# Transposing K loads of 3 MB instead of 1 MB, with another load order, in a two-problem attention kernel

## The chip, the cores and the metric

The kernel runs on one core of a Trainium2 chip. The metric is device time in microseconds (us); smaller is better. Ratios compare a kernel with the kernel before on the same chip in the same rounds, because the kernel before has a median of 1126.6 us on one chip and 1133.0 us on another. Where the text compares microseconds of two experiments, they may come from different chips.

A *unit* is one (batch, head) pair of one problem. There are 512 of them, 256 of problem A and then 256 of problem B. A *group* is four units. One group's K is 1 MB and its V is 1 MB.

## The reference, cut to what matters

```python
# two times (A, B) with B=16, Sq=144, D=448, H=16, Sk=512, Dh=256, bf16:
q = (x @ wq).reshape(B, Sq, H, Dh).transpose(0, 2, 1, 3)
scores = jnp.einsum("bhqd,bhkd->bhqk", q, k_cache) * (Dh ** -0.5)
p = softmax(scores, axis=-1)
o = jnp.einsum("bhqk,bhkd->bhqd", p, v_cache)
out = o.transpose(0, 2, 1, 3).reshape(B, Sq, H * Dh) @ wo
# the two outputs are concatenated along the last axis
```

The data are 134 MB of K and as much V, each byte used once, and some 19 MB of x, wq and wo.

## The kernel before: the parts that matter

One unit is eight matmuls for Q, eight for the scores S, an exponential on ScalarE, eight matmuls for PV, one for the row sums, and a normalization into a ring, from which the output projection (OP) takes chunks of 128 rows. TensorE works on Q of unit i+6, S of unit i+2 and PV of unit i in turn. All large loads are issued in order from one queue (SyncE, "SPq" in the profile):

```python
LQ, LS = 6, 2
WAVE = 4
NK, NV, NXG = 6, 5, 2                     # ring slots for K groups, V groups, x
kt_sb = sb("kt_sb", [128, NK, 8, UG * 128], BF16)

def t_load_k(G):                          # 1 MB: 512 rows of 1024, transposed by the DMA
    pr, r0 = divmod(UG * G, NU)
    sl = G % NK
    src = ks[pr].rearrange("b h (p c) d -> (b h p) (c d)", c=4)[r0 * 128:(r0 + UG) * 128, :]
    def e(q):
        return q.dma_start_transpose(kt_sb[:, sl, :, :], src).then_inc(sems["kt%d" % sl], 16)
    S.add(SP, e, writes=[(("kt", sl), G)], dma_sem="kt%d" % sl, name="k%d" % G)
# ... t_load_v(G): a plain 1 MB load into v_sb[:, G % NV]
# order: sorted by deadline. The first four groups one by one, then waves: K of four groups, then V of four.
for G in range(NG):
    lo = UG * (G - NK) + UG - 1 - LS + 1 if G >= NK else s_min     # when the slot is free
    w = 1 if G < WAVE else WAVE
    plan(lo, UG * (G - G % w) - LS, 0, 10 ** 6, t_load_k, G)
# ... the same for V, and for x, wq and wo by their deadlines
```

The columns of wq for problem B can be loaded only after the last Q of problem A that uses them, and wo of B only after the last output chunk of A. So about 7 MB of extra loads fall into the switch from A to B.

## Time and profile before

| | before |
|---|---|
| three runs without profile | 1123.84, 1124.79, 1131.62 us |
| profiled run | 1134.42 us (span 1132.7) |
| TensorE busy | 1050.6 us, 93% |
| undisturbed pace | 2.03 us per unit |

First the head of the profile page: the span, the engine table, and TensorE and the DMA engines in 40 slices of the span, each digit a busy share in tenths.

```profile
span 1132.7 us, 33125 instructions
...
PE 1050.6 (93%) x13952; PEld 925.9 (82%) x13952; DVE 657.6 (58%) x2183; ACT 621.8 (55%) x1573; POOL 643.4 (57%) x1065
...
PE   4857999999999999999969989999999999999995
...
DMA  9999999999999999999999999999999999999930
```

TensorE has two holes, the first 10% and the middle, where B begins. The DMA engines have none until the very end. Both are nearly full, so the question is which of them is waited for, and where. The waits view (total us, times, longest us) says that in the holes TensorE waits for DMA:

```profile
PE ot_ps L1007 <- DMA v_sb<-in_A_v_cache_dram: 22.1, 5, 12.7
PE qp_ps L937 <- DMA wq_sb<-in_A_wq_dram: 16.9, 3, 10.6
PE qp_ps L937 <- DMA wq_sb<-in_B_wq_dram: 10.9, 2, 7.4
...
PE ot_ps L1007 <- DMA v_sb<-in_B_v_cache_dram: 7.1, 3, 4.3
...
PE s_ps L961 <- DMA kt_sb<-in_A_k_cache_dram: 1.6, 1, 1.6
```

What a K load costs is seen in short windows. The last three columns are TensorE's granted clock, the DMA share and GB/s:

```profile
52.00:54.00 2.00, 2.00 (x35) 1.99 (x33) 1.41 (x6) 1.47 (x4) 1.38 (x3) 1.00 1.28 290
54.00:56.00 2.00, 0.91 (x12) 0.53 (x9) 1.51 (x5) 0.88 (x3) 1.38 (x3) 1.00 1.22 129
64.00:66.00 2.00, 0.00 (x0) 0.00 (x0) 0.00 (x0) 0.00 (x0) 0.00 (x0) 0.50 0.65 141
66.00:68.00 2.00, 0.00 (x0) 0.00 (x0) 0.00 (x0) 0.00 (x0) 0.00 (x0) 0.50 1.27 290
72.00:74.00 2.00, 0.62 (x6) 0.62 (x7) 0.00 (x0) 0.00 (x0) 0.00 (x0) 0.50 1.05 405
```

From 49.5 to 68.5 us four K loads run back to back. They move at 290 GB/s, but with windows between that move half of it: 4.8 us per load, where 1 MB at 290 GB/s would take 3.6. A share of the DMA near 1 does not tell these apart; the GB/s do. Plain V traffic (72 to 74 us) reaches 405. The clock of 0.50 is the other price of a long wait: eight matmuls took 1.14 us after it, 0.66 us otherwise. The Trainium skill ("TensorE: Matmul & The Clock Gate", Part 1: The HAM clock gate) says that an idle window brings the array to half clock; this trace agrees.

The queue's own timeline (start, length; issue times) shows those loads:

```profile
45.20 22.11 SPq L913 DMA_TRANSPOSE kt_sb<-in_A_k_cache_dram  x4
67.36 2.52 SPq L922 DMA_DIRECT2D v_sb<-in_A_v_cache_dram  x4
```

### The profile page before, as it was taken

The page shows a single profiled execution, that of the slowest core. Times are in us where ns is not written, and L with a number is a line of the kernel's source. Part 1 is how long each engine was busy: PE and PEld are TensorE (multiplying, and loading weights), DVE is VectorE, ACT ScalarE, POOL GpSimd, SP SyncE. Part 2 cuts the span into 40 slices and gives each one's busy share as a digit, 9 for nine tenths or more (in the row PEclk, how much of TensorE's full clock was granted, in tenths as well). Part 3 has the DMA queues.
Part 4 walks back from the last instruction along what each step waited for, and adds up shares of the span by engine and source line. Part 5 has one row for each costly group of instructions (what it writes and reads, how often), then busy time and mean ns, then how long its engine had stood idle before and what let it go on. Part 6 is the DMA issues. An engine that isn't in the chain of part 4 may idle for free.

```text
span 1132.7 us, 33125 instructions
## 1 busy us (share of the span) xinstructions
PE 1050.6 (93%) x13952; PEld 925.9 (82%) x13952; DVE 657.6 (58%) x2183; ACT 621.8 (55%) x1573; POOL 643.4 (57%) x1065
## 2 busy tenths in 40 slices
PE   4857999999999999999969989999999999999995
PEld 3756888888888888888858878888888888888883
DVE  2534566666656666666526645666656665666653
ACT  1534555665655555656525545666655555565552
POOL 1535456666656656666526645666656665666652
PEclk9879999999999999999979999999999999999998
DMA  9999999999999999999999999999999999999930
GB/s 239 255 310 258 267 285 273 279 275 285 256 270 262 277 274 264 261 270 240 268 309 282 254 270 265 284 279 283 229 262 263 281 274 282 283 264 261 264 121 12
DMA packets 629087, 294.21 MB, mean 260 GB/s; under 512 B 550464, under 2 KB 558656, under 8 KB 628928
## 3 DMA queue, kind: packets, MB, share of 16 engines
q1 hardware_dynamic: 627200, 287.86, 107.5%
q0 software_dynamic: 1728, 4.13, 1.0%
q8 instruction: 111, 1.82, 0.7%
q14 instruction: 48, 0.39, 0.1%
HBM read 148.90 MB, written 4.13 MB: 135 GB/s over the span
## 4 chain that ended last, share of the span: by engine, by line
PE 74%; DVE 7%; DMA 7%; SPq 6%; ACT 5%; issue 1%; POOLq 0%; POOL 0%; ACTq 0%
PE qp_ps L937 19%; PE op_ps L1098 18%; PE s_ps L961 18%; PE ot_ps L1007 16%; SPq L913 5%; ACT pt_sb L973 4%; DVE run_sb L1063 3%; DMA v_sb<-in_A_v_cache_dram 3%; DVE ring L1050 2%; DVE qt_sb L949 2%; PE ot_ps L1019 2%; DMA v_sb<-in_B_v_cache_dram 2%; DMA wq_sb<-in_B_wq_dram 1%; ACT ln_sb L1030 1%; DMA kt_sb<-in_A_k_cache_dram 1%
## 5 line engine op out<-in xcount | busy, mean ns | idle before, releaser
L982 POOL TENSOR_TENSOR pp_sb<-pt_sb 128x288 f32<-128x288 bf16 x512 | 374.3, 731 | 433.9 <-ACT pt_sb L973 433.0
L973 ACT ACTIVATE pt_sb<-s_ps 128x576 bf16<-128x576 f32 x512 | 333.4, 651 | 438.2 <-PE s_ps L961 438.1
L1063 DVE TENSOR_REDUCE run_sb<-ot_ps 1x1 bf16<-1x144 f32 x1024 | 262.2, 293 | 376.5 <-ACT ln_sb L1030 376.5
L937 PE MATMUL qp_ps<-xt_sb,wq_sb 128*128 128x144 bf16 x4096 | 347.3, 229 | 38.6 <-DMA wq_sb<-in_A_wq_dram 16.9
L937 PEld LDWEIGHTS qp_ps<-xt_sb,wq_sb 128*128 128x128 bf16 x4096 | 284.3, 99 | 113.2 <-issue 29.7
L1007 PE MATMUL ot_ps<-pt_sb,v_sb 128*128 128x144 bf16 x4096 | 344.1, 228 | 29.2 <-DMA v_sb<-in_A_v_cache_dram 22.1
L961 PE MATMUL s_ps<-qt_sb,kt_sb 128*128 128x144 bf16 x4096 | 344.6, 228 | 1.6 <-DMA kt_sb<-in_A_k_cache_dram 1.6
L1007 PEld LDWEIGHTS ot_ps<-pt_sb,v_sb 128*128 128x128 bf16 x4096 | 277.8, 99 | 31.1 <-DMA v_sb<-in_A_v_cache_dram 23.0
L961 PEld LDWEIGHTS s_ps<-qt_sb,kt_sb 128*128 128x128 bf16 x4096 | 278.5, 99 | 2.6 <-DMA kt_sb<-in_A_k_cache_dram 1.8
L949 DVE CAST qt_sb<-qp_ps 128x288 bf16<-128x288 f32 x512 | 225.5, 441 | 86.1 <-PE qp_ps L937 82.8
L986 POOL TENSOR_TENSOR ps_sb<-pp_sb 128x144 bf16<-128x144 f32 x512 | 250.6, 489 | 40.2
L1098 PE MATMUL op_ps<-wo_sb,ring 128*128 128x448 bf16 x1120 | 265.5, 353 | 0.5 <-DVE ring L1050 0.5
L1050 DVE TENSOR_TENSOR ring<-ot_ps,rinv_sb 128x288 bf16<-128x288 f32 (+8 forms) x640 | 231.0, 375 | 0.0
L1035 ACT ACTIVATE rinv_sb<-ln_sb 128x144 f32<-128x144 f32 x512 | 165.4, 323 | 16.1
L1030 ACT ACTIVATE ln_sb<-ot_ps 128x144 f32<-128x144 f32 x512 | 149.1, 291 | 35.0 <-PE ot_ps L1019 34.8
L1098 PEld LDWEIGHTS op_ps<-wo_sb,ring 128*128 128x128 bf16 x1120 | 98.2, 98 | 44.5 <-DVE ring L1050 1.1
L1019 PE MATMUL ot_ps<-ps_sb,ones 128*128 128x144 bf16 x512 | 116.3, 227 | 0.0
L1019 PEld LDWEIGHTS ot_ps<-ps_sb,ones 128*128 128x128 bf16 x512 | 50.5, 99 | 0.0
L1116 ACT ACTIVATE ost_sb<-op_ps 128x448 bf16<-128x448 f32 x35 | 18.6, 531 | 8.7 <-PE op_ps L1098 8.6
L1127 POOL DMA_DIRECT2D out_dram<-ost_sb x36 | 20.2, 561 | 4.3 <-ACT ost_sb L1116 4.1
L1098 PE MATMUL qp_ps<-wo_sb,ring 128*128 128x448 bf16 x32 | 7.2, 352 | 0.0
L1098 PEld LDWEIGHTS qp_ps<-wo_sb,ring 128*128 128x128 bf16 x32 | 3.1, 98 | 2.9
(13 smaller groups left out, 6.1 us busy)
## 6 DMA issues: line engine op xcount, KB each, us to landing
v_sb<-in_A_v_cache_dram SPq DMA_DIRECT2D x64, 1024.0 KB, 9.6
v_sb<-in_B_v_cache_dram SPq DMA_DIRECT2D x64, 1024.0 KB, 10.1
out_dram<-ost_sb POOLq DMA_DIRECT2D x36, 112.0 KB, 4.8
wo_sb<-in_A_wo_dram SPq DMA_DIRECT2D x8, 448.0 KB, 9.1
wo_sb<-in_B_wo_dram SPq DMA_DIRECT2D x8, 448.0 KB, 5.0
wq_sb<-in_A_wq_dram SPq DMA_DIRECT2D x4, 768.0 KB, 5.6
wq_sb<-in_B_wq_dram SPq DMA_DIRECT2D x4, 768.0 KB, 14.0
kt_sb<-in_A_k_cache_dram SPq DMA_TRANSPOSE x64, 7.9
```

What stands on the lines that cost most here:

```text
L937: ins = t.matmul(qp_ps[:, dc * SQ:(dc + 1) * SQ], lhsT=wq_sb[:, kc, c0:c0 + 128], rhs=xt_sb[:, xsl, kc, xo:xo + SQ], start=(kc == 0 and dc ...
L949: return v.tensor_copy(qt_sb[:, sl, :, :], src)
L961: ins = t.matmul(s_ps[bank][:, c // 2, (c % 2) * SQ:(c % 2 + 1) * SQ], lhsT=kt_sb[:, ksl, 2 * c + dc, jj * 128:(jj + 1) * 128], rhs=qt_sb[ ...
L973: return a.activation(pt_sb[:, psl, :, :].rearrange("p (a b) q -> p a (b q)", a=2), s_ps[bank][:, :, 0:2 * SQ], AF.Exp, scale=DH ** -0.5)
L982: return g.tensor_tensor(pp_sb[:, sl, :, :], pt_sb[:, psl, 0:2, :], pt_sb[:, psl, 2:4, :], op=ALU.add)
L986: return g.tensor_tensor(ps_sb[:, sl, :], pp_sb[:, sl, 0, :], pp_sb[:, sl, 1, :], op=ALU.add)
L1007: ins = t.matmul(ot_ps[ob][:, dc * SQ:(dc + 1) * SQ], lhsT=v_sb[:, vsl, j, c * DH + dc * 128:c * DH + (dc + 1) * 128], rhs=pt_sb[:, sl, c, ...
L1019: return t.matmul(ot_ps[ob][:, 2 * SQ:3 * SQ], lhsT=ones[:, :], rhs=ps_sb[:, sl, :], start=True, stop=True)
L1035: return a.activation(rinv_sb[:, sl, :], ln, AF.Exp, scale=-1.0)
L1050: ins = v.tensor_tensor(ring[:, 2 * h:2 * h + 2, r0:r0 + q1 - q0], ot_ps[ob][:, 0:2 * SQ].rearrange("p (c q) -> p c q", c=2)[:, :, q0:q1], ...
L1063: return v.tensor_reduce(run_sb[0:1, k, U:U + 1], ot_ps[ob][0:1, 2 * SQ:3 * SQ], axis=AX.X, op=op)
L1098: ins = t.matmul(acc[0:m, 0:D], lhsT=ring[:, c, col0:col0 + m], rhs=wo_sb[:, c, :], start=(c == first), stop=(c == last))
```

## The change

K of up to three groups comes in one transposing load of 3 MB. The layout of `kt_sb` changes so that the slots lie side by side along the free dimension. Each such load is followed by the V loads of the same groups, with wq between them where it is due. The intent is fewer K loads and a better order at the switch. The turns from K to V traffic do not become fewer: in the steady stretch they come every 12 units instead of every 16.

```diff
-    WAVE = 4
+    WAVE, NKD = 3, 4
-        kt_sb = sb("kt_sb", [128, NK, 8, UG * 128], BF16)
+        kt_sb = sb("kt_sb", [128, 8, NK * UG * 128], BF16)
-        def t_load_k(G):
+        def t_load_k(G, m):
-            src = ks[pr].rearrange("b h (p c) d -> (b h p) (c d)", c=4)[r0 * 128:(r0 + UG) * 128, :]
+            src = ks[pr].rearrange("b h (p c) d -> (b h p) (c d)", c=4)[r0 * 128:(r0 + m * UG) * 128, :]
+            sem = "kt%d" % (k_index[G] % NKD)
-                return q.dma_start_transpose(kt_sb[:, sl, :, :], src).then_inc(sems["kt%d" % sl], 16)
+                return q.dma_start_transpose(kt_sb[:, :, sl * UG * 128:(sl + m) * UG * 128], src).then_inc(
+                    sems[sem], 16)
# ... matmul operand and semaphores to match; the sorting by deadline goes, and instead:
+        while G < NG:
+            n = min(WAVE, NG - G)
+            # ... x, when it is due
+            while g < G + n:
+                m = min(G + n - g, NK - g % NK, GPP - g % GPP)
+                k_index[g] = len(k_index)
+                plan(t_load_k, g, m)
+                g += m
+            for g in range(G, G + n):
+                pr, gl = divmod(g, GPP)
+                if gl < HG:
+                    plan(t_load_wq, pr, gl)
+                plan(t_load_v, g)
+                if pr == 0 and gl == WAVE * 2 - 1:
+                    for wg in range(NWG):
+                        plan(t_load_wo, 0, wg)
+            G += n
```

More of the change, by code (lines that the diff above doesn't have):

```diff
@@ L839, in bass_concat_heads__mha_block_cached__gqa_block_cached__near_ridge_kernel @@
         sem_names = list(COMPUTE)
-        for i in range(NK):
+        for i in range(NKD):
             sem_names.append("kt%d" % i)
@@ L905, in t_load_x @@
             S.add(SP, e, writes=[(("xt", sl), XG)], dma_sem="xt%d" % sl, n_dma=2, name="x%d" % XG)
-        def t_load_k(G):
+        def t_load_k(G, m):
             pr, r0 = divmod(UG * G, NU)
             sl = G % NK
-            src = ks[pr].rearrange("b h (p c) d -> (b h p) (c d)", c=4)[r0 * 128:(r0 + UG) * 128, :]
+            src = ks[pr].rearrange("b h (p c) d -> (b h p) (c d)", c=4)[r0 * 128:(r0 + m * UG) * 128, :]
+            sem = "kt%d" % (k_index[G] % NKD)
             def e(q):
-                return q.dma_start_transpose(kt_sb[:, sl, :, :], src).then_inc(sems["kt%d" % sl], 16)
-            S.add(SP, e, writes=[(("kt", sl), G)], dma_sem="kt%d" % sl, name="k%d" % G)
+                return q.dma_start_transpose(kt_sb[:, :, sl * UG * 128:(sl + m) * UG * 128], src).then_inc(
+                    sems[sem], 16)
+            S.add(SP, e, writes=[(("kt", sl + j), G + j) for j in range(m)], dma_sem=sem, name="k%d" % G)
         def t_load_v(G):
@@ L961, in e @@
                         ins = t.matmul(s_ps[bank][:, c // 2, (c % 2) * SQ:(c % 2 + 1) * SQ],
-                                       lhsT=kt_sb[:, ksl, 2 * c + dc, jj * 128:(jj + 1) * 128],
+                                       lhsT=kt_sb[:, 2 * c + dc, (ksl * UG + jj) * 128:(ksl * UG + jj + 1) * 128],
                                        rhs=qt_sb[:, U % NQT, dc, :], start=(dc == 0), stop=(dc == 1))
@@ L1131, in bass_concat_heads__mha_block_cached__gqa_block_cached__near_ridge_kernel @@
         t_init()
+        s_min = -LQ - 24
         dma_plan = []
-        def plan(lo, deadline, phase, lead, fn, *args):
-            dma_plan.append((deadline, phase, len(dma_plan), lo, lead, fn, args))
-        s_min = -LQ - 24
-        def wave(G):
-            return UG * (G - G % WAVE)
-        for XG in range(NXGT):
-            pr, j = divmod(XG, Bn // XB)
-            u_first = pr * NU + j * XB * H
-            if XG >= NXG:
-                pr0, j0 = divmod(XG - NXG, Bn // XB)
-                lo = pr0 * NU + (j0 + 1) * XB * H - 1 - LQ + 1
+        _at = [s_min]
@@ new lines, in plan @@
+        def plan(fn, *args):
+            if fn is t_load_x:
+                XG = args[0]
+                pr0, j0 = divmod(XG - NXG, Bn // XB)
+                lo = pr0 * NU + (j0 + 1) * XB * H - LQ if XG >= NXG else s_min
+            elif fn is t_load_wq:
+                pr, hg = args
+                lo = pr * NU - H + 4 * hg + 4 - LQ if pr > 0 else s_min
+            elif fn is t_load_k:
+                lo = UG * (args[0] + args[1] - NK) - LS if args[0] + args[1] > NK else s_min
+            elif fn is t_load_v:
+                lo = UG * (args[0] - NV + 1) if args[0] >= NV else s_min
@@ L1148, in bass_concat_heads__mha_block_cached__gqa_block_cached__near_ridge_kernel @@
             else:
                 lo = s_min
-            plan(lo, u_first - LQ - 16, 0, 10 ** 6, t_load_x, XG)
-        for pr in range(NP):
-            for hg in range(HG):
-                dl = pr * NU + 4 * hg - LQ
-                lo = pr * NU - H + 4 * hg + 3 - LQ + 1 if pr > 0 else s_min
-                plan(lo, dl, 1, 10 ** 6, t_load_wq, pr, hg)
-        for wg in range(NWG):
-            plan(s_min, OP_START - 12 + wg, 2, 10 ** 6, t_load_wo, 0, wg)
-        for G in range(NG):
-            lo = UG * (G - NK) + UG - 1 - LS + 1 if G >= NK else s_min
-            w = 1 if G < WAVE else WAVE
-            plan(lo, UG * (G - G % w) - LS, 0, 10 ** 6, t_load_k, G)
@@ L1162, in bass_concat_heads__mha_block_cached__gqa_block_cached__near_ridge_kernel @@
-        for G in range(NG):
-            lo = UG * (G - NV) + UG - 1 + 1 if G >= NV else s_min
-            w = 1 if G < WAVE else WAVE
-            plan(lo, UG * (G - G % w) - LS, 1, 10 ** 6, t_load_v, G)
-        dma_plan.sort(key=lambda t: t[:3])
-        _prev = s_min
-        _tmp = []
-        for dl, ph, sq, lo, lead, fn, args in dma_plan:
-            _prev = max(_prev, lo, dl - lead)
-            _tmp.append((_prev, dl, sq, fn, args))
-        dma_plan = _tmp
+            _at[0] = max(_at[0], lo)
@@ new lines, in plan @@
+            dma_plan.append((_at[0], fn, args))
+        k_index = {}
+        GPP = NG // NP
+        x_next = 0
+        G = 0
+        while G < NG:
+            n = min(WAVE, NG - G)
+            while x_next < NXGT and UG * (G + n) > x_next * XB * H - H:
+                plan(t_load_x, x_next)
+                x_next += 1
+            g = G
+            while g < G + n:
[12 more added lines that the diff above has]
+            G += n
@@ L1210, in bass_concat_heads__mha_block_cached__gqa_block_cached__near_ridge_kernel @@
             while dma_plan and dma_plan[0][0] <= i:
-                _sl, _dl, _sq, fn, args = dma_plan.pop(0)
+                _lo, fn, args = dma_plan.pop(0)
                 fn(*args)
```

## The prediction

> **What bounds the kernel now.** Two resources nearly tie. TensorE is busy 1050.6 of 1132.7 us (engine table). Undisturbed, by the starts of the 512 exponentials (one per unit), units 64 to 152 take 178.5 us and 320 to 456 take 276.9: 2.03 us per unit. DMA needs almost as long. In windows of 2 us, transposing traffic peaks at 290 GB/s (3.6 us per 1 MB K load), but in four back-to-back K loads from 49.5 to 68.5 us each takes about 4.8 us: 1.1 us of near-silence per load. V runs at 370 to 400 GB/s, 2.7 us per load; a switch from K to V costs about 2 us. A wave of 16 units is 4x4.8 + 4x2.7 + 2 = 32 us of DMA against 32.5 of TensorE. Any extra load (x, wq, wo) becomes a TensorE wait.
>
> Waits (wait view): V 29.2 us, wq 27.8 (10.6 is the start), K 1.6; 29.7 more is put down to issue. Two places lose: the first 120 us (12.7 us at 61, 6.5 at 108, 4.6 at 26), and 532 to 694 us, where units 232 to 344 take 252.9 us against 227: wq of problem B stands behind slot-bound K loads, V behind wo.
>
> **What the change does.** The bytes stay. Two thirds of the per-load gaps go: 3 MB should take 3x3.6 + 1.1 = 12 us instead of 14.3, if 290 GB/s holds inside one load. A wave of 12 units then needs 12 + 8.2 + 2 = 22 us against 24.4 of TensorE: 10% DMA slack instead of 2%. The Trainium skill ("DMA: Bandwidth & Descriptors", Latency and other measured facts) has 261 GB/s for a non-contiguous DMA transpose; this trace's 290 within a load decides.
>
> Price: the first wq now stands behind 3 MB of K, until about 22 us: the first Q moves from 10.6 to 22 us, the first exponential from 20.7 to 30; unit 12's Q waits for the fourth wq until about 54 us. The waits at 61 and 108 us go. Exponential 40 starts near 122 us instead of 129.9: 8 us gained.
>
> At the switch to B, wq is laid between single V loads; one 5 us wait is left (third wq behind 3 MB of K), so 19 us gained. Smaller V waits (142, 270, 815 us) go: 1 us. The pace of 2.03 us and the tail stay: TensorE's.
>
> **Sum.** 1124.8 - 8 - 19 - 1 = 1097; leaning towards a worse start, 1100 us. Range 1078 to 1120. Chances: faster over 2% 0.58, within 2% 0.38, slower 0.04.
>
> **What would show it.** 3 MB K loads landing in about 13 us, transposing traffic flat at 290 GB/s. First Q near 22 us, first exponential near 30, a wait for wq until about 54, exponential 40 near 122. Units 232 to 344 in about 234 us. V waits below 5 us in total. Units 64 to 152 still 178 us.
>
> **What would make it wrong.** The 1.1 us gaps recur within a 3 MB load (14 to 15 us each): no slack, the start 10 us worse, near 1115. Or slots freed 12 units at a time stall K: my margin is 24 us against 12 to 15. After long waits TensorE's clock falls (0.56 from 62 to 73 us; eight matmuls then took 1.14 instead of 0.66 us; the skill's "TensorE: Matmul & The Clock Gate", Part 1, ties it to idle windows): fewer, longer waits move a few us. The switch may stall on wo, which shares K's queue.

## The result, and the profile after

| | before | after |
|---|---|---|
| runs | 1123.84, 1124.79, 1128.40, 1131.62 us | 1112.11, 1112.30, 1113.43, 1113.96 us |
| median | 1126.6 us | 1112.87 us |
| ratio | | 0.9874 (95%: 0.9834 to 0.9913) |

The kernel is 1.3% faster: inside the range of the prediction, but within 2%, where I had put the larger chance on more. That it lies inside owes much to a range of 42 us: of the 28 us that I had summed up, half came. On another chip, against before's 1131.5 us, the same kernel had 1113.4 us and a ratio of 0.9835 (0.9777 to 0.9892). The kernel after is also steadier: its eight runs span 4.4 us, the kernel before's seven on that second chip alone span 11.

The head of the page after:

```profile
span 1112.2 us, 33041 instructions
...
PE 1044.0 (94%) x13952; PEld 920.7 (83%) x13952; DVE 657.3 (59%) x2183; ACT 620.2 (56%) x1573; POOL 642.2 (58%) x1065
...
PE   1698999999999999999969999999999999999995
...
DMA  9999999999999999999999999999999999999930
```

The waits view after:

```profile
PE qp_ps L939 <- DMA wq_sb<-in_A_wq_dram: 32.5, 2, 22.7
...
PE qp_ps L939 <- DMA wq_sb<-in_B_wq_dram: 9.6, 1, 9.6
...
PE s_ps L963 <- DMA kt_sb<-in_A_k_cache_dram: 3.2, 1, 3.2
...
PE op_ps L1100 <- DMA wo_sb<-in_B_wo_dram: 0.8, 1, 0.8
```

No wait for V is left. All waits of TensorE for DMA together were 58.6 us before and 46.1 us after (55.0 and 46.0 in the second profiles shown below). One long wait at the start has become longer (22.7 us, the first wq behind 3 MB of K), one of 9.6 us at the switch remains. The windows after show what a 3 MB load looks like:

```profile
12.00:14.00 2.00, 0.00 (x0) 0.00 (x0) 0.00 (x0) 0.00 (x0) 0.00 (x0) 1.00 1.28 290
14.00:16.00 2.00, 0.00 (x0) 0.00 (x0) 0.00 (x0) 0.00 (x0) 0.00 (x0) 1.00 1.28 290
38.00:40.00 2.00, 2.00 (x35) 1.99 (x33) 1.41 (x6) 1.34 (x4) 1.39 (x3) 1.00 2.14 275
40.00:42.00 2.00, 1.91 (x31) 1.72 (x28) 1.64 (x6) 1.35 (x4) 1.51 (x3) 1.00 0.53 116
42.00:44.00 2.00, 1.75 (x29) 1.56 (x26) 1.24 (x4) 1.61 (x5) 1.26 (x3) 1.00 1.27 290
```

The first load runs flat at 290 GB/s. The second (35 to 48 us) has a silence in its middle, at 40 us, where no load begins or ends. That was not in my picture, and it is taken up below.

To see where the time went I use the start of each unit's exponential (one instruction per unit, 512 in all). Two profiles of each kernel are shown; the second of before is the first experiment, the second of after comes from the second chip. Times are us from the span's start.

| exponential of unit | before | before, 2nd | after | after, 2nd |
|---|---|---|---|---|
| 0 | 20.7 | 21.9 | 31.6 | 30.8 |
| 40 | 129.9 | 130.3 | 126.2 | 123.6 |
| 64 | 177.2 | 177.2 | 173.1 | 170.5 |
| 232 | 517.8 | 517.7 | 512.8 | 510.3 |
| 344 | 770.7 | 764.7 | 752.1 | 750.7 |
| 511 | 1115.0 | 1108.9 | 1095.7 | 1094.3 |
| span | 1132.7 | 1125.6 | 1112.2 | 1111.6 |

From the second profile of before to the first of after the span falls by 13.4 us (the medians fall by 13.7): 4.1 us by unit 64, 0.8 us from 64 to 232, 7.7 us from 232 to 344 (the switch: 247.0 to 239.3), 0.6 us from 344 to 511, and 0.2 us after. The pace of the undisturbed stretches does not move: units 64 to 152 take 178.3 us in that second profile of before and 177.5 in after.

### The profile page after: what moved, and what is told of

Read it like the earlier page. It is cut to its first block, busy times and chain, and to the rows that moved or that the text cites. A ratio compares the mean times of both kernels' runs of the same rounds, so it can differ in the third digit from the quotient of the medians.

```text
span 1112.2 us, 33041 instructions
## 1 busy us (share of the span) xinstructions
PE 1044.0 (94%) x13952; PEld 920.7 (83%) x13952; DVE 657.3 (59%) x2183; ACT 620.2 (56%) x1573; POOL 642.2 (58%) x1065
## 4 chain that ended last, share of the span: by engine, by line
PE 76%; DVE 8%; ACT 6%; SPq 4%; DMA 4%; issue 1%; POOLq 0%; POOL 0%; ACTq 0%
PE qp_ps L939 20%; PE s_ps L963 19%; PE op_ps L1100 19%; PE ot_ps L1009 16%; ACT pt_sb L975 4%; SPq L914 3%; DVE run_sb L1065 3%; DVE ring L1052 2%; DVE qt_sb L951 2%; PE ot_ps L1021 2%; DMA kt_sb<-in_A_k_cache_dram 2%; ACT ln_sb L1032 1%; DMA wo_sb<-in_B_wo_dram 1%; DMA wq_sb<-in_A_wq_dram 1%; DMA wq_sb<-in_B_wq_dram 0%
```

## The experiments

Eleven runs were made, nine of them of changed kernels; all gave correct results. Two ideas for more lookahead were not run. A ring of eight K slots with 4 MB loads does not fit into the on-chip memory SBUF (the build stops at `qt_sb`: 3456 bytes needed where 2912 were left). With fewer V slots and a shorter output ring it fitted, but then an output chunk was overwritten before it was read, and the kernel did not build.

### The kernel before, once more

No edit.

> The kernel before, unchanged, for a second profile. The first profile ran 1134.4 us, 8 to 10 us over the median of the unprofiled runs. Theory: the kernel before sits on a tie of DMA and TensorE, so its waits for V around 640 to 700 us (4.3 + 2.3 us) and after the x loads come and go from run to run; this profile then shows 1124 to 1128 us and fewer such waits. Rival: the profile itself costs some 8 us; then this one is near 1134 too.

It took 1127.37 us, with a profile of 1125.6 us, against 1127.4 to 1136.7 us of the unprofiled runs on its chip. So the profile does not cost 8 us, and the rival is out. The waits of this profile:

```profile
PE ot_ps L1007 <- DMA v_sb<-in_A_v_cache_dram: 19.6, 3, 12.4
PE qp_ps L937 <- DMA wq_sb<-in_B_wq_dram: 9.8, 2, 6.6
...
PE ot_ps L1007 <- DMA v_sb<-in_B_v_cache_dram: 4.4, 2, 3.8
```

The V waits of A and B are 24.0 us instead of 29.2, and units 232 to 344 took 247.0 us instead of 252.9. The first profile was of one of the less lucky runs of a kernel whose time wanders, and I had subtracted what I saw in it from the median of others.

### Order without size

```diff
-                plan(t_load_k, g, m)
+                plan(None, g, m)              # only advances the time, as for the 3 MB load
+                for j in range(m):
+                    k_index[g + j] = len(k_index)
+                    plan(t_load_k, g + j, 1)
# ... NKD = 6 semaphores, and plan(None, ...) enters no load
```

> The kernel after with each 3 MB K load cut into three 1 MB loads back to back, all else and the order unchanged. Theory A (each K load has a fixed 1.1 us of silence, so size gives the DMA slack): three loads take 14.3 us where one took 12, DMA needs 24.5 us per 12 units against TensorE's 24.4, V or K waits come back in the steady stretch and the start is 5 to 10 us worse: 1120 us or more. Theory B (the silences come from instruction fetches that fall into transposing traffic, whatever the load size, and the gain comes from the order of the loads alone): 1113 us, and the V waits stay at zero.

It took 1125.9 us (1124.3 to 1130.4), ratio to before 0.9955 (0.9909 to 1.0000). Theory B falls: the order alone is worth 0.45%, and by the interval between nothing and 0.9%. The profile (1125.6 us) shows that it trades: unit 64 comes at 171.6 us, 5.6 us earlier than in the kernel before, but units 232 to 344 take 249.1 us against 247.0, and units 344 to 511 346.6 against 344.2. V and wo waits are back:

```profile
PE qp_ps L939 <- DMA wq_sb<-in_B_wq_dram: 11.1, 1, 11.1
...
PE op_ps L1100 <- DMA wo_sb<-in_B_wo_dram: 3.4, 2, 1.9
...
PE ot_ps L1009 <- DMA v_sb<-in_B_v_cache_dram: 2.8, 2, 2.4
PE ot_ps L1009 <- DMA v_sb<-in_A_v_cache_dram: 2.5, 2, 1.4
```

The start, though, is no worse than with 3 MB loads (171.6 against 173.1 and 170.5), so the part of theory A that had it 5 to 10 us worse falls too. One thing is not quite equal: the first of three small loads may start when its own slot is free, a large one only when all three are. That favours the small loads, and they lose all the same.

### Size without order

The kernel before, its order kept, with the layout of after and 2 MB loads in the waves:

```diff
-            plan(lo, UG * (G - G % w) - LS, 0, 10 ** 6, t_load_k, G)
+            m = 1 if G < WAVE else 2
+            if G % m:
+                continue
+            lo = UG * (G + m - NK) - LS if G + m > NK else s_min
+            plan(lo, UG * (G - G % w) - LS, 0, 10 ** 6, t_load_k, G, m)
```

> The kernel before with the order of before, but the K loads of a wave of 16 units in two 2 MB loads instead of four 1 MB loads. Theory A: two fixed silences of 1.1 us per wave fewer, 4 to 8 us faster than before (1118 to 1122). Theory B: same as before within its spread (1124 to 1130); the wait for wq of problem B stays over 10 us in both.

It took 1115.0 us (1114.7 to 1115.3), ratio 0.9855 (0.9819 to 0.9891). This is 16 to 18 us, more than twice the 4 to 8 us that theory A had asked for; why it is so much more stays open. Merging pairs of loads in the old order gives, within the intervals, what the whole change gives. With the run before, which had the new layout but small loads, this settles the main question: the gain comes from the size of the K loads. TensorE's waits for DMA agree: 55.1 us together with the order alone, 39.0 us with the size alone.

```profile
PE s_ps L962 <- DMA kt_sb<-in_A_k_cache_dram: 8.0, 2, 5.6
...
PE ot_ps L1008 <- DMA v_sb<-in_A_v_cache_dram: 5.9, 3, 4.7
PE qp_ps L938 <- DMA wq_sb<-in_B_wq_dram: 5.9, 2, 3.9
...
PE ot_ps L1008 <- DMA v_sb<-in_B_v_cache_dram: 2.2, 1, 2.2
```

The wait for wq of B fell to 5.9 us, although I had expected it to stay over 10. I read this as wq arriving earlier, because the K loads ahead of it take less DMA time.

What a load takes, from the trace's packet records (first to last packet of each K load that started after 120 us; worked out from the records, not a line of a view):

| kernel | size | loads | mean us | median us |
|---|---|---|---|---|
| before | 1 MB | 116 | 4.99 | 4.98 |
| order without size | 1 MB | 116 | 5.01 | 4.98 |
| size without order | 2 MB | 58 | 9.37 | 9.24 |
| after | 3 MB | 36 | 13.39 | 13.04 |

A line through the means of 1 and 3 MB (5.01 and 13.39) is 4.19 us per MB and 0.82 us per load; it gives 9.2 us for 2 MB. So a 3 MB load saves 2 x 0.82 = 1.6 us, not 2.3 us as I had it. The 0.82 us are a fit, and not all of it need be the load's own. With small loads in the new order, the 14 loads with no instruction-fetch packet (see below) from 0.5 us before their start to their end took 4.1 us on average, the 72 with one took 5.2 us. A short load meets fewer packets anyway, so the split stays open.

The K loads begun after 120 us take 588 us together with small loads in the new order, and 510 us in the kernel after. Part of this shows as a quiet load queue. In steps of 0.2 us in which the packets that begin on it carry less than 10 GB/s, it is quiet for 16.4 us between 120 and 520 us with small loads in the new order, and for 29.8 us in the kernel after; between 700 and 1040 us it is 14.2 and 24.6 us. (Packets still under way do not count here: with the bytes of all queues spread over each packet's duration, 0.0 and 8.6, and 0.2 and 7.6 us are left.) The last load's data end at 1087.3 and 1064.1 us. Only 13 us of all that reach the time, since TensorE sets the pace in between.

### The wq loads of B before the large K load

```diff
-                if gl < HG:
+                if gl < HG and (pr == 0 or g < G0 + 2):
                     plan(t_load_wq, pr, gl)
                 plan(t_load_v, g)
+                if g == G0 + 1:
+                    for hg in range(2, HG):
+                        plan(t_load_wq, 1, hg)
```

> The kernel after with the third and fourth wq load of problem B put before the 3 MB K load of units 264 to 275 instead of behind it. Theory: the wait of 9.6 us at 577 us and the slow clock after it go, about 12 us faster than after: 1101 us; units 256 to 264 take 16 us instead of 28.2. Rival: the K load, 6 us later, becomes the next wait and half of it is given back: 1106 us.

It took 1111.5 us (1110.2 to 1114.2), ratio 0.9832 (0.9792 to 0.9871); the kernel after, unchanged, has 0.9874 and 0.9835 on its two chips. So this is the same as after: not only the theory fell but the rival as well, as more than half was given back. The wait for wq is gone, and others have come:

```profile
PE s_ps L963 <- DMA kt_sb<-in_B_k_cache_dram: 4.7, 2, 3.3
...
PE s_ps L963 <- DMA kt_sb<-in_A_k_cache_dram: 3.8, 1, 3.8
...
PE op_ps L1100 <- DMA wo_sb<-in_B_wo_dram: 2.6, 1, 2.6
```

Units 256 to 264 took 20.4 us instead of 28.2, but units 232 to 344 took 238.2 us, against 240.4 us in the second profile of after. Moving one load in a crowded queue moved the wait.

### The kernel after on the second chip, and added instructions

The second profile of after was taken with two kernels that carry some 12,500 instructions more. These are waits on a semaphore that has long passed, after the first 60 instructions of each engine. They do nothing but must be fetched. (12,500 was my count beforehand. The traces have 40,024 instructions instead of 33,041 and 40,108 instead of 33,125, so 6,983 more.)

```diff
+        PAD = {ACT: 3, DVE: 2, POOL: 4}
+                    for _ in range(PAD.get(eng_name, 0)):
+                        eng.wait_ge(table[PE], 1)
```

> The kernel after, unchanged, on the same chip as the other runs of this job: 1111 to 1115 us. In its trace the 3 MB K loads take 13.0 us (median, first to last packet).

It took 1113.4 us (1112.6 to 1116.5); the 3 MB loads had a median of 13.2 us and a mean of 13.38.

> The kernel after with some 12,500 more instructions (waits on a semaphore that has long passed, on ScalarE, VectorE and GpSimd), which do nothing but have to be fetched. Theory (each 16 KB instruction fetch stops transposing traffic for about 1.3 us, which is part of what I took for a fixed cost per load): some 40 to 50 more fetch packets, and a 3 MB K load takes 13.5 us or more instead of 13.0. Its time stays within 10 us of after, as after has DMA slack outside the start and the switch. Rival (fetches only coincide with the silences): K loads stay at 13.0 us.

> The same added instructions in the kernel with 1 MB loads, which has no DMA slack. Theory: K loads go from 4.9 to 5.1 us or more each, and the time rises by more than in the kernel after, to over 1135 us. Rival: 1124 to 1131 us as without them.

The reason for this pair is the silence at 40 us. The packet records of the kernel after show packets of 16 KB on the instruction queues, and where one falls into transposing traffic, that traffic goes silent shortly after. Of the 45 such packets that began well inside a K load (0.3 us after its start or later, 1.5 us before its end or earlier), all 45 were followed within 1.2 us by a silence of 0.5 us or more (transposing packets begun at under 40 GB/s); of 11 packets of 8 KB, 6 were. The first 130 us have four cases of 16 KB:

```
16 KB instruction packet at 39.4  77.4  99.45 120.78 us
silence of transposing traffic from 39.9 (1.3), 77.9 (1.2), 99.9 (1.4), 121.2 (1.4) us
```

The queue table of the second profile of after, then of the one with more instructions (packets, MB, share):

```profile
q8 instruction: 111, 1.82, 0.7%
q14 instruction: 48, 0.39, 0.1%
```

```profile
q8 instruction: 111, 1.82, 0.6%
q14 instruction: 103, 0.84, 0.2%
```

There are 55 more packets, all of 8 KB on queue 14; the 16 KB packets stay at 111. So this tests the small packets, and for the large ones there is only the coincidence in time. The fetch packets per 3 MB load (from its first packet to the end of its last) rise from 1.89 to 2.97 (mean), and the load from 13.38 to 14.08 us (median 13.2 to 13.7). Within the padded kernel, loads with one fetch take 12.8 us (median of 5), with two 13.7 (6), with three 13.7 (13), with four 15.0 (9). A fetch more in a 3 MB load thus goes with some 0.65 us more. Each side is one run, but this side of the theory held.

The other did not. In the kernel with 1 MB loads, fetches per load rose from 0.85 to 1.32 by the same count, but the mean load went only from 5.01 to 5.07 us, less than expected. Nor do the times say what I wanted: 1131.7 and 1141.0 us, 18 and 15 us above their bases (the second base is a median from another chip), the first far beyond the 10 us that I had allowed. The added instructions slowed the undisturbed stretch as well (units 64 to 152: 181.0 us against 177.6 in the second profile of after), so these times say nothing about DMA. What the runs show is that large transposing loads were longer where more fetches fell into them. How much of the time before the change was due to them stays open.

### Another start

```diff
-            n = min(WAVE, NG - G)
+            n = min(1 if G < WAVE else WAVE, NG - G)
+                if g == WAVE:
+                    plan(t_load_wq, 0, WAVE)        # the fourth wq ahead of the fourth K group
-                if gl < HG:
+                if gl < HG and g != WAVE:
-                if pr == 0 and gl == WAVE * 2 - 1:
+                if pr == 0 and gl == WAVE * 3 - 1:  # wo three groups later
```

> The kernel after with another start: the first three groups in 1 MB K loads, each followed by its wq and V, the fourth wq before the fourth K load, and wo of problem A behind the ninth V instead of behind the sixth. Theory: the first Q is back at 10.6 us and the wait for the fourth wq goes; then DMA bounds the first 120 us, and exponential 64 starts 3 to 8 us earlier than after's 173 us: 1105 to 1110 us. Rival: the start is DMA-bound whatever the order, exponential 64 stays at 171 to 173 us and the time at 1112 us.

It took 1113.05 us (1112.5 to 1114.9), the kernel after 1113.36 on the same chip: the rival was right. The first exponential came at 27.1 us and exponential 40 at 118.8 us, 4.8 us ahead of the second profile of after. By exponential 64 nothing was left: 170.5 us in both. K waits took it:

```profile
PE qp_ps L939 <- DMA wq_sb<-in_A_wq_dram: 23.2, 3, 14.5
...
PE s_ps L963 <- DMA kt_sb<-in_A_k_cache_dram: 9.6, 4, 4.2
```

My reading is that the start depends on how long the DMA needs for what the first 64 units use, and that this comes out the same in these two orders.

### wo of B later

On top of the moved wq loads, four loads of wo from unit 270 and four from unit 282, and the first output chunk of B begun at unit 290:

```diff
-                            queue_chunk(r, max(i + OP_DELAY, OP_START))
+                            queue_chunk(r, max(i + OP_DELAY, OP_START + pr * (NU + 4)))
+            while wo_free and i >= NU + (14 if wo_n < 4 else 26):
+                t_load_wo(1, wo_free.pop(0))
+                wo_n += 1
```

> The kernel with wq of problem B moved ahead (as in s3), and besides wo of problem B loaded later: four loads from unit 270, four from unit 282 on, with the first output chunk of B begun at unit 290 instead of 273. Theory (the switch is bound by the sum of DMA work that falls into it, so that moving one load only moves the wait; spreading it into later slack is what helps): units 240 to 320 take 6 us less than the 176.3 us of after: 1105 to 1108 us. Rival: what is put off is missed later, by unit 344 nothing is gained: 1111 us as s3.

It took 1112.8 us (1111.4 to 1116.4), ratio 0.9863 (0.9819 to 0.9908): the rival. Units 240 to 320 took 175.7 us, in the second profile of after 176.3. No order that I tried at the switch made it shorter by more than about 2 us.

### Where along the run the size pays

Small loads everywhere but in groups 48 to 83, and the reverse:

```diff
-                k_index[g] = len(k_index)
-                plan(t_load_k, g, m)
+                plan(None, g, m)                      # only advances the time, as above
+                st = 1 if not 48 <= G < 84 else m     # and the reverse: 48 <= G < 84
+                for j in range(0, m, st):
+                    k_index[g + j] = len(k_index)
+                    plan(t_load_k, g + j, st)
```

> The kernel after with 1 MB K loads everywhere but in groups 48 to 83 (units 192 to 335, around the switch to problem B), where they stay at 3 MB. Theory: the DMA time that large loads save is worth something only where wq and wo of B crowd the queue, so 10 of the 13 us between s1_split and after stay: 1114 to 1118 us. Rival: the saving counts evenly over the whole run; with 36 of 128 groups in large loads only a quarter of it stays: 1122 to 1124 us.

> The reverse: 1 MB K loads only in groups 48 to 83, 3 MB elsewhere. Theory: most of the gain of large loads is gone: 1120 to 1126 us, with the loss between units 240 and 304. Rival: three quarters of it stay: 1115 to 1117 us.

Large loads only around the switch took 1119.8 us (1116.2 to 1122.5), large loads everywhere else 1115.6 us (1113.1 to 1117.3). My theory, that the saving counts only at the switch, falls. With 36 of 128 groups about half of the 13 us stay, with the other 92 about four fifths. The rival fits the second but not quite the first. The shares are rough: both kernels spread over some 4 to 6 us and ran on a chip without the other two, and the ratios to before (0.9898, 0.9840 to 0.9957, and 0.9863, 0.9807 to 0.9918) overlap.

The traces say why it is not local. With large loads only around the switch, unit 256 comes 8.4 us later than with small loads only there (566.0 and 557.6 us). Units 248 to 256, still at the edge of the switch, took 21.9 us against 14.9, though these groups are loaded in 3 MB. I read this as a queue that comes to the switch with less lead, with less slack before it (the load queue quiet, by the count above, for 23.4 us between 120 and 520 us, in the reverse kernel 25.8, in the kernel after 29.8); the lead itself I did not measure, so this stays a reading. With small loads at the switch and large ones before it, the loss is later: units 288 to 304 took 36.3 us, in the second profile of after 33.0.

## Why the prediction was right or wrong

- **Both resources nearly tie, and large loads give the DMA slack: right.** The wait view had no V wait left (29.2 us before), the load queue was quiet about twice as long in the steady stretches, and the two runs that separate order and size put the gain on size (0.9955 for order alone, 0.9855 for size alone).
- **Undisturbed pace unchanged: right.** Units 64 to 152 were predicted at 178 us and took 177.5.
- **"3 MB should take 3x3.6 + 1.1 = 12 us": mis-sized.** It took 13.0 us (median) to 13.4 (mean). The 1.1 us per load that I had read off four loads were about 0.8 us per load. What I took for one cost of the load also holds silences after instruction fetches, of which both kernels have 159 packets however many loads there are.
- **The start.** The shape was right point by point: first Q predicted at 22 us, measured 22.7; first exponential 30 and 31.6; wait for the fourth wq until 54 and 53.6. "Exponential 40 starts near 122 us: 8 us gained" was mis-sized: 126.2 and 123.6 us, 4 to 7 us gained. A K wait of 3.2 us, ended at 86 us, was not in my list.
- **The switch: "19 us gained" was the largest error.** It has two parts. I expected 234 us for units 232 to 344, and they took 239.3: the wait for wq was 9.6 us instead of 5, with slow clock after it. And the 252.9 us that I subtracted from belonged to a run of 1134 us, while the second profile has 247.0. Against that one the gain is 7.7 us.
- **The sum: the step that failed was "1124.8 - 8 - 19 - 1".** It takes the losses of a profiled run of 1134.4 us from a median of 1124.8. Between the second profile of before (1125.6) and after (1112.2) the terms are 4.1 + 7.7 + 1.6 = 13.4 us. Of the 14.6 us by which my 28 us were too many, 5.9 are the unlucky profile, 5.3 the switch after the change and 3.9 the start; the other terms came out 0.6 us better than predicted. (The two profiles are from two chips.)
- **The order as a cause of the gain at the switch: wrong.** I had put those 19 us down to wq lying between V loads. The new order with small loads has no gain there (249.1 us against 247.0), the old order with larger loads has one: unit 232 at 513.0 and unit 344 at 752.9 us, 239.9 us.

## What to carry to other kernels

Where DMA and TensorE nearly tie, take a fixed cost out of the most frequent load before rearranging the queue: here every order tried with 3 MB loads came out within about 2 us of the others, while merging 1 MB transposing loads into larger ones gave 1 to 1.5%. The saving is not paid out evenly in time: of 78 us less spent in K loads only 13 us reached the time, most of it at the start and the crowded switch. And when a kernel's times wander by 1%, take a second profile before subtracting waits: a profile is one run, and its waits must be subtracted from its own time.

## What the Trainium skill lacked or had wrong

- "DMA: Bandwidth & Descriptors", Latency and other measured facts, has 261 GB/s as the effective rate of a non-contiguous DMA transpose. Here transposing traffic ran flat at 290 GB/s inside a load; over whole loads it was 210 GB/s at 1 MB (1.049 MB in 4.99 us) and 235 at 3 MB (3.146 MB in 13.39 us). The page gives no load size, and a second, higher figure for a contiguous transpose; which of its two cases these loads are was not tested.
- The same page, Rules for kernel authors, advises to coalesce and calls 1 MiB and more good for maximum bandwidth. For transposing loads 1 MiB was not enough: merging two or three saved about 0.8 us for each load less, and about 13 us of this kernel's time.
- No page has it that transposing DMA traffic goes silent after instruction fetches. Here all 45 packets of 16 KB inside a K load were followed by a silence, of 1.2 to 1.4 us in the four cases listed, and one 8 KB packet more per 3 MB load went with 0.65 us more. "DMA: Bandwidth & Descriptors", Queues, rings and completion order, where it would belong, only says that an engine takes turns between queues packet by packet.
- "TensorE: Matmul & The Clock Gate", Part 1, agreed: granted clock 0.50 after a long wait, eight matmuls in 1.14 us instead of 0.66.
